# Three weight loads moved from block 1 to block 8 of the first stage

## The chip, the cores and the metric

The kernel runs on one core of one Trainium2 chip. The metric is the time of one execution on the device, in microseconds. A run also leaves a profile of one execution, from which all rows below come. The engines are called as the profile calls them: PE (matmuls; PEld is its weight load), DVE (vector), ACT (scalar activation), POOL (GpSimd) and SP (SyncE), whose only work here is to issue DMAs.

## What is computed

The reference is the sum of an input `x` (2048 tokens of 512, bf16), a sliding-block attention and a gated MLP that mixes tokens, both on the same normalized `x`:

```python
xn = _layernorm(x)
# attention, 32 heads of 16, window of 256 tokens
q, k, v = split(xn @ wqkv)
p = softmax(where(mask, q @ k.T * 16 ** -0.5, -1e9))
a = (p @ v) @ wo
# gated MLP
z = gelu(xn @ w_in)                  # 2048 x 1376
z1, z2 = z[..., :688], _layernorm(z[..., 688:])
g = w_sp @ z2 + b_sp[:, None]        # mixes the 2048 tokens
out = x + a + (z1 * g) @ w_out
```

The bias is `b_sp` (2048 values), `wo` is 512x512, and `w_out` is 688x512.

## The kernel before

The 2048 tokens are 16 blocks of 128 rows (`n` from 0 to 15; `b` is the group of four blocks, `j` the place in the group). There are two stages.

The first stage is the loop over `n` at L392. For each block, PE makes the two halves of `z` (`z_half`, L325, matmuls at L333) from the transposed normalized input `xnT`, and some units of the q, k, v projection (`qkv_unit`, L124, matmuls at L131 and L149, tiles `pj_o` and `pj_f`). ACT applies the gelu and copies q and k out; DVE does the layer-norm statistics (`bn_stats`), normalizes (`ln_apply`, L286 to L293, giving `xn`), copies v out and normalizes `z2`. `xnT` is made by `transposes` (L311 and L312): one transposing DMA for each block, issued by SP, which reads `xn` and writes the block's columns of `xnT`. Four buffers hold `xn`. Blocks 0 to 3 of `xnT` are also needed early and are partly made on PE; from block 4 on PE reads what the DMA wrote.

The second stage runs from an order written out by hand (`ORDER`, L61): token mixing (`gf`, L496), attention scores and products (`S`, L641 and L584), and the output products `fo`, six with `w_out_sb` (L531) and four with `wo_sb` (L538) for each block. The bias is used there as `b_all`, a float copy of `b_bf` made at L441 at the end of the first stage.

Every engine runs its instructions in program order, and SP too: a DMA that waits, for its input or for the queue, holds all DMAs behind it. Completion semaphores for DMAs are eight lanes used in turn, so a DMA also waits until the one eight places ahead has landed. SP's order in the first stage is: the inputs and `w_in`, `x` of blocks 4 to 7 and `wqkv`; transposes of blocks 0, 1, 4 and 5; then, in `load_late` (L223), called once in block 1, `x` of blocks 8 to 15, the bias, `wo` and the first 640 rows of `w_out`; transposes of 6 and 7 (called in block 3); the last 48 rows of `w_out` (L235, in `setup_late`, called in block 4, behind a DVE memset of that chunk); then transposes of 8 and 9 (block 6), 10 and 11 (block 7), 12 and 13 (block 10), 14 and 15 (block 11). The next DMAs are the first loads of the second stage (L477).

The bias load reads 2048 values of 2 bytes so that token `n*128 + p` goes to partition `p`, column `n`:

```python
nc.sync.dma_start(out=b_bf[:], in_=B_b_sp.rearrange("(n p) -> p n", p=P))
```

Of the kernel before, what the change touches and what calls it, by code (L numbers as in the profile page):

```python
# [75 lines left out]
def kernel(  # L76
# [12 lines left out]
    nc = tc.nc  # L89
# [12 lines left out]
    w_out_sb = pers.tile([P, NFC, D], BF, name="w_out_sb")  # L102
# [21 lines left out]
    def qkv_unit(b, i, k):  # L124
        t0 = b * 512
        pt = bank(k)
        if i < 8:
            G, isk = divmod(i, 2)
            w0 = isk * D + G * P
            for c in range(NC):  # L130
                nc.tensor.matmul(  # L131
                    pt[:], lhsT=wqkv[:, c, w0 : w0 + P], rhs=xnT[:, c, t0 : t0 + 512],
                    start=(c == 0), stop=(c == NC - 1),
                )
                yield 512
            if isk:
                nc.scalar.copy(out=kT[:, G, t0 : t0 + 512], in_=pt[:])
            else:
                qt = psum["qt"].tile([P, 512], BF, name="qt", bufs=2)
                nc.scalar.copy(out=qt[:], in_=pt[:])  # L140
                for e in range(2):
                    nc.vector.tensor_scalar(  # L142
                        out=qpad[b][:, G, e, :], in0=qt[:],
                        scalar1=hmask[:, e : e + 1], scalar2=None, op0=ALU.mult,
                    )
        else:
            m = 4 * b + i - 8
            for c in range(NC):
                nc.tensor.matmul(  # L149
                    pt[:], lhsT=xnT[:, c, m * P : (m + 1) * P], rhs=wqkv[:, c, 2 * D : 3 * D],  # L150
                    start=(c == 0), stop=(c == NC - 1),
                )
                yield 512
            nc.vector.tensor_copy(
                out=v_y[:, m, 0 : H * VW].rearrange("p (h w) -> p h w", w=VW)[:, :, 0:DH],
                in_=pt[:].rearrange("p (h d) -> p h d", d=DH),
            )
# [4 lines left out]
    with ExitStack() as actx:  # L162
# [13 lines left out]
        def load_x(eng, n0, n1):  # L176
            b, j = divmod(n0, 4)
            eng.dma_start(
                out=xts[b][:, j : j + n1 - n0, :],
                in_=x2[n0 * P : n1 * P, :].rearrange("(j p) d -> p j d", p=P),  # L180
            )
# [22 lines left out]
        def warm_up(k):  # L204
# [13 lines left out]
            out=hmask[:],  # L218
            in_=ident[:].rearrange("p (s e d) -> p e s d", s=4, e=2),
# [3 lines left out]
        def load_late():  # L223
            load_x(nc.sync, 8, 12)
            load_x(nc.sync, 12, 16)
            with nc.allow_non_contiguous_dma(reason="tiny bias gather"):
                nc.sync.dma_start(out=b_bf[:], in_=B_b_sp.rearrange("(n p) -> p n", p=P))
            nc.sync.dma_start(out=wo_sb[:], in_=A_wo.rearrange("(c p) n -> p c n", p=P))
            nc.sync.dma_start(
                out=w_out_sb[:, 0:5, :], in_=B_w_out[0:640, :].rearrange("(c p) n -> p c n", p=P)  # L230
            )

        def setup_late():
            nc.vector.memset(w_out_sb[:, NFC - 1, :], 0.0)
            nc.sync.dma_start(out=w_out_sb[0:48, 5, :], in_=B_w_out[640:688, :])  # L235
            nc.vector.memset(v_y[:, :, H * VW : VROW], 0.0)
            ones = v_y[:, :, 0 : H * VW].rearrange("p m (h w) -> p m h w", w=VW)
            nc.vector.memset(ones[:, :, :, DH : DH + 1], 1.0)
# [3 lines left out]
        for h in range(2):  # L242
            part = slice(h * KB, h * KB + KB)
            nc.gpsimd.affine_select(
                out=maskFD[part, 0, :], in_=maskFD[part, 0, :], pattern=[[-1, KB]],
# [3 lines left out]
                out=maskFD[part, 1, :], in_=maskFD[part, 1, :], pattern=[[1, KB]],  # L249
# [26 lines left out]
        def ln_batch(b0, k):  # L276
            mvt = sm.tile([P, 4, 2], F32, name="mvt")
            for n in range(b0, b0 + k):
                ln_stats(n, b0, mvt)
                if n == b0 + k - 1:  # L280
                    rs = rstd(mvt, k)
                    for m in range(b0, b0 + k):
                        rsx[m] = rs[:, m - b0 : m - b0 + 1]
                yield

        def ln_apply(n, name="xn"):  # L286
            xs = xts[n // 4][:, n % 4, :]
            xn = lt.tile([P, D], BF, name=name, bufs=4 if name == "xn" else EARLY)
            nc.vector.tensor_scalar(  # L289
                out=xn[:], in0=xs, scalar1=mvx[n], scalar2=rsx[n],  # L290
                op0=ALU.subtract, op1=ALU.mult,
            )
            return xn  # L293
# [17 lines left out]
        def transposes(n, xn):  # L311
            nc.sync.dma_start_transpose(out=xnT[:, :, n * P : (n + 1) * P], in_=xn[:])  # L312
# [12 lines left out]
        def z_half(n, half, inside=None):  # L325
            zp = ps_s.tile([P, 2, 512], F32, name="zp", tag="S")
            src = xcT[:, n] if n < EARLY else xnT[:, :, n * P : (n + 1) * P]
            for c in range(NC):
                if c == NC // 2 and inside is not None:
                    inside()  # L330
                for j in range(2):
                    f0 = half * FH + j * HALF
                    nc.tensor.matmul(  # L333
                        zp[:, j, 0:HALF], lhsT=src[:, c, :],
                        rhs=w_in_sb[:, c, f0 : f0 + HALF],
                        start=(c == 0), stop=(c == NC - 1),
                    )
            dst = (z1 if half == 0 else z2n)[:, n, :]
            nc.scalar.activation(  # L339
                out=dst.rearrange("p (j f) -> p j f", j=2),  # L340
                in_=zp[:, :, 0:HALF], func=ACT.Gelu_apprx_tanh,
                scale=rsx[n] if n < EARLY else 1.0,
            )
# [3 lines left out]
        def z_stats(n):  # L347
            if n % 2 == 0:
                zmv[n // 2] = sm.tile([P, 4, 2], F32, name="zmv")
            mvt = zmv[n // 2]  # L350
            st = sm.tile([P, 2, nc.vector.BN_STATS_DIM], F32, name="st2")
            for j in range(2):
                nc.vector.bn_stats(out=st[:, j, :], in_=z2n[:, n, j * HALF : (j + 1) * HALF])  # L353
            nc.vector.bn_aggr(out=mvt[:, n % 2, :], in_=st[:])
            if n % 2 == 1:
                return rstd(mvt, 2)
            return None
# [34 lines left out]
        for n in range(NB):  # L392
            b, j = divmod(n, 4)
            if n > 1:
                z_half(n, 0)
            if n == 4:
                setup_late()
            if b < 3:
                if j < 2:
                    for i, _ in enumerate(ln_batch(4 * b + 4 + 2 * j, 2)):  # L400
                        if n == 1 and i == 0:
                            for k in (4, 5):
                                transposes(k, ln_apply(k))
                            load_late()
                elif n != 2:
                    for m in range(2):
                        k = 4 * b + 4 + 2 * (j - 2) + m
                        transposes(k, ln_apply(k))
            if n >= 1 and n != 3:
                r = z_stats(n - 1)  # L410
                if r is not None:
                    z_rs[n - 1] = r
            ks = "ofof"[: QKV_AT.get(n, 0)]
            if 3 < n < NB - 1:
                for k in ks[0:1]:
                    for _ in qkv_unit(*qkv_list.pop(0), k):
                        pass
                ks = ks[1:]
            z_half(n, 1, inside=(lambda: turn_early(2, xns.pop(2), 1)) if n == 1 else None)
            if n == 1:  # L420
                turn_early(3, xns.pop(3), 1)
            if n == 3:
                for k in ks[0:2]:
                    for _ in qkv_unit(*qkv_list.pop(0), k):
                        pass
                ks = ks[2:]
                z_stats(n - 1)
            if n % 2 == 1 and n >= 3:
                r = z_rs[n - 2]
                z_apply(n - 3, r)  # L430
                z_apply(n - 2, r)
            if n == NB - 1:
                r = z_stats(n)
            for i, k in enumerate(ks):
                for _ in qkv_unit(*qkv_list.pop(0), k):
                    pass
            if n == NB - 1:
                nc.scalar.activation(out=warm[:, 0:4], in_=warm[:, 4:8], func=ACT.Exp)
                z_apply(n - 1, r)
                z_apply(n, r)  # L440
                nc.vector.tensor_copy(out=b_all[:], in_=b_bf[:])  # L441
# [471 lines left out]
```

## Time and profile before

| | us |
|---|---|
| median of 3 runs | 256.01 |
| lowest and highest of them | 255.07, 257.02 |
| the profiled execution | 254.87 |
| its span, first to last instruction | 253.0 |
| PE, ACT, DVE busy in the span | 246.8, 191.2, 178.6 |
| granted PE clock | 1.0 throughout |

The first stage ends for PE around 86 us; the second takes the rest of the span. Rows of a timeline give start and length in us, engine, line and what is written from what; a bracket gives the idle time ahead of the row and what ended it. A row of waits gives who waited for whom, the total, how often and the longest. SPq rows show how long SP was occupied with issuing a DMA, not how long the transfer took; the time to landing is a separate figure.

### The profile page before, as it was taken

The numbers are of one execution on the slowest core, as the hardware profiler recorded it, in microseconds if no ns is written. First come the engines' busy times: TensorE is split into PE (matmuls) and PEld (weight loads), VectorE is DVE, ScalarE is ACT, GpSimd is POOL, SyncE is SP. The second block draws the span as 40 slices with busy tenths as digits, with TensorE's granted clock in tenths as the row PEclk, the third lists the DMA queues.
The fourth block names the chain that finished last, engine by engine and source line by source line (L and its number), as shares of the span: only waits on it lengthen the run. The fifth ranks groups of instructions, "written<-read, shape, count | busy, mean of one in ns | idle before, by whom it ended". The sixth has DMA issues, their size and how long they took to land.

```text
span 253.0 us, 9066 instructions
## 1 busy us (share of the span) xinstructions
PE 246.8 (98%) x4012; PEld 136.1 (54%) x4036; DVE 178.6 (71%) x373; ACT 191.2 (76%) x229; POOL 16.9 (7%) x53
## 2 busy tenths in 40 slices
PE   8999999999999999999999999999999999999995
PEld 3655555555555455555564555546455555556553
DVE  4997997974557738829586955349688766858974
ACT  6756656546446989989789898989988989988900
POOL 3320312111011000000000000000000000000000
PEclk9999999999999999999999999999999999999999
DMA  6998541039102117783944725445724517852452
GB/s 221 393 165 198 149 81 4 5 65 151 32 0 76 36 20 100 147 89 81 159 89 98 176 51 127 89 99 124 136 85 80 141 34 119 158 99 65 34 90 75
DMA packets 68026, 26.16 MB, mean 103 GB/s; under 512 B 57056, under 2 KB 67472, under 8 KB 67984
## 3 DMA queue, kind: packets, MB, share of 16 engines
q1 hardware_dynamic: 67408, 25.12, 49.0%
q8 instruction: 32, 0.52, 0.9%
q10 hardware_dynamic: 576, 0.44, 0.6%
q14 instruction: 10, 0.08, 0.1%
HBM read 8.41 MB, written 2.10 MB: 42 GB/s over the span
## 4 chain that ended last, share of the span: by engine, by line
PE 87%; DVE 6%; DMA 4%; issue 2%; SPq 1%; POOL 0%; POOLq 0%
PE gf L496 32%; PE S L641 11%; PE zp L333 9%; PE S L584 8%; PE fo L531 8%; PE fo L538 5%; PE pj_o L131 5%; PE pj_f L131 4%; PE pj_f L149 3%; DMA xnT<-xn 2%; PE pj_o L149 2%; DMA xt<-in_A_x_dram 2%; DVE stats L259 1%; DVE st L353 1%; DVE xn L289 1%
## 5 line engine op out<-in xcount | busy, mean ns | idle before, releaser
L650 ACT ACTIVATE E<-S 128x1024 bf16<-128x1024 f32 x152 | 141.9, 1018 | 14.4 <-PE S L641 13.5
L496 PE MATMUL gf<-z2n,wspT 128*128 128x344 bf16 x512 | 85.7, 310 | 0.0
L496 PEld LDWEIGHTS <-wspT 128*128 128x128 bf16 x512 | 45.5, 98 | 31.8 <-issue 11.3
L669 DVE TENSOR_TENSOR E<-E,maskFD 128x1024 bf16<-128x1024 bf16 (+2 forms) x48 | 38.2, 810 | 8.3 <-ACT E L650 7.8
L333 PE MATMUL zp<-w_in_sb,xnT 128*128 128x344 bf16 x224 | 36.6, 309 | 0.2 <-DMA xnT<-xn 0.2
L641 PE MATMUL S<-qpad,kT 32*64 32x512 bf16 (+3 forms) x960 | 31.9, 309 | 0.1
L591 DVE STREAM_TRANSPOSE ot<-S 128x1024 f32<-128x1024 f32 x16 | 20.0, 1247 | 14.4 <-PE S L584 14.3
L333 PEld LDWEIGHTS <-xnT 128*128 128x128 bf16 x224 | 21.8, 98 | 14.3 <-DMA xnT<-xn 0.7
L502 DVE SCALAR_TENSOR_TENSOR u<-gf,b_all,z 128x344 bf16<-128x344 f32 x32 | 18.2, 567 | 12.8 <-PE gf L496 11.5
L531 PE MATMUL fo<-w_out_sb,uT 128*128 128x512 bf16 (+2 forms) x90 | 23.3, 366 | 1.0 <-issue 0.6
L641 PEld LDWEIGHTS <-kT 32*64 32x64 bf16 x960 | 10.9, 102 | 21.6 <-issue 20.6
L584 PE MATMUL S<-E,v_y 64*32 64x256 bf16 (+2 forms) x960 | 21.5, 231 | 0.0
L584 PE MATMUL S<-E,vx 64*32 64x256 bf16 (+3 forms) x960 | 21.5, 232 | 0.0
L339 ACT ACTIVATE z<-zp 128x688 bf16<-128x688 f32 x14 | 10.4, 743 | 14.2 <-PE zp L333 14.1
L584 PEld LDWEIGHTS <-vx 64*32 64x32 bf16 x960 | 18.1, 90 | 4.5 <-issue 4.4
L552 DVE TENSOR_TENSOR xo<-fo,xo 128x512 bf16<-128x512 f32 (+2 forms) x17 | 11.1, 654 | 13.0 <-PE fo L538 12.9
L131 PEld LDWEIGHTS <-wqkv 128*128 128x128 bf16 x128 | 12.5, 98 | 12.6
L584 PEld LDWEIGHTS <-v_y 64*32 64x32 bf16 x960 | 18.9, 90 | 0.6 <-issue 0.6
L131 PE MATMUL pj_o<-xnT,wqkv 128*128 128x512 bf16 x71 | 18.9, 379 | 0.2
L142 DVE TENSOR_SCALAR qpad<-qt,hmask 128x512 bf16<-128x512 bf16 x32 | 9.7, 344 | 10.5 <-ACT qt L140 10.5
L339 ACT ACTIVATE z2n<-zp 128x688 bf16<-128x688 f32 x14 | 10.4, 743 | 8.8 <-PE zp L333 8.8
L538 PE MATMUL fo<-wo_sb,oT 128*128 128x512 bf16 (+2 forms) x64 | 16.3, 366 | 0.6 <-issue 0.6
(70 smaller groups left out, 206.4 us busy)
## 6 DMA issues: line engine op xcount, KB each, us to landing
xo<-in_A_x_dram SPq DMA_DIRECT2D x16, 128.0 KB, 3.1
out_dram<-xo SPq DMA_DIRECT2D x15, 128.0 KB, 2.6
vx<-v_y SPq DMA_DIRECT2D x16, 102.0 KB, 2.7
xt<-in_A_x_dram SPq DMA_DIRECT2D x3, 512.0 KB, 6.1
wqkv<-in_A_wqkv_dram SPq DMA_DIRECT2D x1, 1536.0 KB, 9.5
w_in_sb<-in_B_w_in_dram SPq DMA_DIRECT2D x3, 344.0 KB, 4.8
w_out_sb<-in_B_w_out_dram SPq DMA_DIRECT2D x1, 640.0 KB, 5.6
wo_sb<-in_A_wo_dram SPq DMA_DIRECT2D x1, 512.0 KB, 7.8
```

What stands on the lines that cost most here:

```text
L131: nc.tensor.matmul(pt[:], lhsT=wqkv[:, c, w0 : w0 + P], rhs=xnT[:, c, t0 : t0 + 512], start=(c == 0), stop=(c == NC - 1),)
L333: nc.tensor.matmul(zp[:, j, 0:HALF], lhsT=src[:, c, :], rhs=w_in_sb[:, c, f0 : f0 + HALF], start=(c == 0), stop=(c == NC - 1),)
L339: nc.scalar.activation(out=dst.rearrange("p (j f) -> p j f", j=2), in_=zp[:, :, 0:HALF], func=ACT.Gelu_apprx_tanh, scale=rsx[n] if n < EAR ...
L496: nc.tensor.matmul(gf[:, 0:HALF], lhsT=wspT[t][:, c, :], rhs=z2n[:, c, j * HALF : (j + 1) * HALF], start=(c == 0), stop=(c == NB - 1),)
L502: nc.vector.scalar_tensor_tensor(out=u[:, j * HALF : (j + 1) * HALF], in0=gf[:, 0:HALF], scalar=b_all[:, t : t + 1], in1=z1[:, t, j * HALF ...
L531: nc.tensor.matmul(fo[:, 0:w], lhsT=uTs[t][:, ch, :], rhs=w_out_sb[:, ch, c0 : c0 + w], start=(ch == 0), stop=False,)
L538: nc.tensor.matmul(fo[:, 0:w], lhsT=oTs[t // 2][:, c, q0 : q0 + P], rhs=wo_sb[:, c, c0 : c0 + w], start=False, stop=(c == NC - 1),)
L584: nc.tensor.matmul(o[32 * s : 32 * s + 32, h, q0 : q0 + ni * KB], lhsT=v, rhs=Et[part, s, e, c0 : c0 + ni * KB], start=(i == 0), stop=(i = ...
L591: nc.vector.transpose(out=ot[:].rearrange("p h b j -> p (h b j)"), in_=o[:].rearrange("p h c -> p (h c)"))
L641: nc.tensor.matmul(o.rearrange("p (e q) -> p e q", e=2)[:, :, c0 - b0 : c0 - b0 + ni * KB], lhsT=kT[32 * s : 32 * s + 32, 2 * g + h, k0 : ...
L650: nc.scalar.activation(out=Et[:, 2 * i : 2 * i + 2, :, b0 : b0 + w].rearrange("p s e q -> p (s e) q"), in_=S[i][:].rearrange("p s (e q) -> ...
L669: nc.vector.tensor_tensor(out=v, in0=v, in1=mask, op=ALU.mult)
```

## The change

The loads of the bias, of `wo` and of `w_out` go out of `load_late` (called in block 1) into a function `load_weights`, called at the top of block 8 after its first half of `z`. The load of the last 48 rows of `w_out` goes from `setup_late` (block 4) into the same function. The `x` loads of blocks 8 to 15 stay where they were. The memset of the last chunk of `w_out_sb` stays in block 4.

```diff
         def load_late():
             load_x(nc.sync, 8, 12)
             load_x(nc.sync, 12, 16)
+
+        def load_weights():
             with nc.allow_non_contiguous_dma(reason="tiny bias gather"):
                 nc.sync.dma_start(out=b_bf[:], in_=B_b_sp.rearrange("(n p) -> p n", p=P))
             nc.sync.dma_start(out=wo_sb[:], in_=A_wo.rearrange("(c p) n -> p c n", p=P))
             nc.sync.dma_start(
                 out=w_out_sb[:, 0:5, :], in_=B_w_out[0:640, :].rearrange("(c p) n -> p c n", p=P)
             )
+            nc.sync.dma_start(out=w_out_sb[0:48, 5, :], in_=B_w_out[640:688, :])

         def setup_late():
             nc.vector.memset(w_out_sb[:, NFC - 1, :], 0.0)
-            nc.sync.dma_start(out=w_out_sb[0:48, 5, :], in_=B_w_out[640:688, :])
             nc.vector.memset(v_y[:, :, H * VW : VROW], 0.0)
...
             if n == 4:
                 setup_late()
+            if n == 8:
+                load_weights()
             if b < 3:
```

In the built program SP's order is then: `x` of blocks 8 to 15, transposes of 6, 7, 8, 9, 10 and 11, bias, `wo`, `w_out` (two loads), transposes of 12 to 15. The instructions of PE, DVE, ACT and POOL keep their order; DVE gets one more wait at the `b_all` copy and PE two more at the first `fo` group.

## The prediction

> **What bounds the kernel now.** I read the page first, then the list of waits of the matmul engine, then its timeline through the first stage, then the SyncE queue beside it. The page gives busy time by engine, and the chain that ended last by engine:
>
> ```profile
> PE 246.8 (98%) x4012; PEld 136.1 (54%) x4036; DVE 178.6 (71%) x373; ACT 191.2 (76%) x229; POOL 16.9 (7%) x53
> ...
> PE 87%; DVE 6%; DMA 4%; issue 2%; SPq 1%; POOL 0%; POOLq 0%
> ```
>
> PE is busy for 246.8 of 253.0 us. Only what lets PE run without a gap can shorten this kernel, so the waits of PE over the whole span come next (who waited for whom: total us, times, longest us):
>
> ```profile
> PE heat L206 <- PEq L897: 0.8, 1, 0.8
> PE fo L538 <- issue: 0.6, 4, 0.2
> PE fo L531 <- issue: 0.6, 4, 0.2
> PE zp L333 <- DMA xnT<-xn: 0.2, 1, 0.2
> PE pj_f L149 <- issue: 0.2, 1, 0.2
> ```
>
> One wait of the five has a DMA behind it: a z product (L333) waited once, 0.2 us, for a transposing DMA. The timeline of PE shows which (start us, length us; a matmul starts before the one ahead of it has ended):
>
> ```profile
> 22.22 1.03 PE L131 MATMUL pj_o<-xnT,wqkv 128*128 128x512 bf16 x4
> 23.08 1.33 PE L333 MATMUL zp<-w_in_sb,xnT 128*128 128x344 bf16 x8
> ...
> 27.14 1.03 PE L131 MATMUL pj_o<-xnT,wqkv 128*128 128x512 bf16 x4
> 28.34 1.34 PE L333 MATMUL zp<-w_in_sb,xnT 128*128 128x344 bf16 x8 [0.17 <-DMA xnT<-xn]
> ...
> 38.20 1.33 PE L333 MATMUL zp<-w_in_sb,xnT 128*128 128x344 bf16 x8
> ...
> 58.75 1.33 PE L333 MATMUL zp<-w_in_sb,xnT 128*128 128x344 bf16 x8
> ```
>
> The z product at 28.34 is the first of block 6; those at 38.20 and 58.75 are the first of blocks 8 and 12 (counting pairs of z products from block 4 on). The listed idle time, 0.17, understates the loss, because pipelined matmuls overlap in the record. In the undisturbed place four pj matmuls are followed by a z product after 23.08 - 22.22 = 0.86 us; here it takes 28.34 - 27.14 = 1.20 us. The wait costs 1.20 - 0.86 = 0.34 us of PE's time.
>
> **What the change removes.** The SyncE queue (SPq: issue time and its length, not the transfer) before that wait:
>
> ```profile
> 15.69 1.79 SPq L178 DMA_DIRECT2D xt<-in_A_x_dram  x2
> 17.52 0.51 SPq L227 DMA_DIRECT2D b_bf<-in_B_b_sp_dram  x1
> 18.07 4.13 SPq L228 DMA_DIRECT2D wo_sb<-in_A_wo_dram  x1
> 22.25 0.51 SPq L229 DMA_DIRECT2D w_out_sb<-in_B_w_out_dram  x1
> 22.86 2.73 SPq L312 DMA_TRANSPOSE xnT<-xn  x2
> 25.67 0.53 SPq L235 DMA_DIRECT2D w_out_sb<-in_B_w_out_dram  x1
> ```
>
> and the DVE work that feeds the two transposes at 22.86 (blocks 6 and 7), with their time from issue to landing:
>
> ```profile
> 16.69 0.73 DVE L289 TENSOR_SCALAR xn<-xt,mvt,rs 128x512 bf16<-128x512 bf16 x2
> ...
> DMA to landing us min/median/max: 4.4/4.9/5.4
> ```
>
> Their input is ready at 16.69 + 0.73 = 17.42, yet they are issued at 22.86: the queue is held by the bias, w_o and w_out loads, above all for the 4.13 us in which the w_o load stands behind the bias load. Then block 6 takes 5.4 us to land, at 28.3, with the w_o and w_out loads ahead of it. After the change SyncE reaches the transpose as soon as the two x loads are issued, at 15.69 + 1.79 = 17.48. With the slowest landing seen, 5.4 us, block 6 is there at 22.9. PE can ask for it at 27.14 + 0.86 = 28.00. That leaves 5 us, so the 0.34 us goes entirely. It cannot go by more: PE has no other wait there.
>
> Next in line once PE runs 0.34 us earlier is block 8. The transposes of blocks 8 to 11, then of 12 to 15, are these (duration in ns, first and last issue), with the landing times of the first group:
>
> ```profile
> L312 SPq DMA_TRANSPOSE xnT<-xn x4: 1189/1204/1220, 31.8 to 36.2; - x4
> ...
> DMA to landing us min/median/max: 2.4/2.9/4.3
> ...
> L312 SPq DMA_TRANSPOSE xnT<-xn x4: 1189/1205/1221, 49.3 to 55.5; - x4
> ```
>
> Block 8 is issued at 31.8 and landed by 36.1 at the latest; PE wants it at 38.20 - 0.34 = 37.86. It is not late.
>
> **What the change adds in the new place.** The four loads now stand in SyncE's queue between the transposes of block 11 and block 12. The last of the former is issued at 36.2 + 1.2 = 37.4, and the next is not issued before 49.3, because DVE has not made its input: a hole of 11.9 us in the queue. What the loads need (KB, us from issue to landing) and how full the hole is (busy of the engines, clock, DMA share, GB/s):
>
> ```profile
> wo_sb<-in_A_wo_dram SPq DMA_DIRECT2D x1, 512.0 KB, 7.8
> w_out_sb<-in_B_w_out_dram SPq DMA_DIRECT2D x1, 640.0 KB, 5.6
> b_bf<-in_B_b_sp_dram SPq DMA_DIRECT2D x1, 4.0 KB, 6.6
> w_out_sb<-in_B_w_out_dram SPq DMA_DIRECT2D x1, 48.0 KB, 3.4
> ...
> 15.69:28.34 12.65, 12.37 (x67) 6.47 (x67) 10.59 (x33) 7.32 (x12) 2.11 (x3) 1.00 0.97 213
> 37.50:49.30 11.80, 11.75 (x68) 6.64 (x68) 9.23 (x29) 7.07 (x11) 2.07 (x3) 1.00 0.13 11
> ```
>
> Their issue takes 0.51 + 4.13 + 0.51 + 0.53 = 5.68 us at the old price, so SyncE is free at 43.1, 6.2 us before it is needed. Their transfers ran before from 17.52 to 25.67 + 3.4 = 29.07, 11.55 us, in a stretch whose DMA share was 0.97; the hole's share is 0.13, so they should take less. Even at 11.55 us they end at 49.0. If block 12 nevertheless landed as slowly as block 6 did, 49.3 + 5.4 = 54.7, PE wants it at 58.75 - 0.34 = 58.41: 3.7 us to spare. Cost on PE: nothing, hidden by that margin.
>
> Who needs the loads, and from when, is in the lines of the first readers (duration in ns, first and last start):
>
> ```profile
> L441 DVE CAST b_all<-b_bf x1: 166/166/166, 83.2 to 83.2; 128x16 f32<-128x16 bf16 x1
> ...
> L531 PE MATMUL fo<-w_out_sb,uT x90: 219/379/390, 106.7 to 249.7; 128*128 128x512 bf16 x78, 128*128 128x384 bf16 x6, 128*128 128x128 bf16 x6
> ...
> L312 SPq EVENT_SEMAPHORE  x14: 17/17/17, 5.3 to 55.4; - x14
> ```
>
> The bias is 34 us early at 83.2, the weights 57 us early at 106.7. In the built program DVE has one more wait ahead of that cast, and PE two more ahead of its first fo group, all on loads long landed; at the 17 ns that such a wait takes on SyncE, an upper 0.05 us, taken as nothing. The orders of PE, ACT, POOL and DVE are otherwise untouched. The Trainium skill, in "DMA: Bandwidth & Descriptors", section "Rules for kernel authors", says to issue a DMA early, compute, and wait on it late, which speaks against moving loads later; by it the move could only cost, and the two rows of first use put that cost at nothing here.
>
> One thing the trace cannot price is whether heavy transfers hold an engine without a named reason. The nearest row is this one, in the middle of the loads' old place:
>
> ```profile
> 23.05 0.48 DVE L238 MEMSET v_y<- 128x512 bf16 x1 [1.72 <-issue]
> ```
>
> DVE stood 1.72 us here for nothing that the profile shows. PE stood for nothing of the sort while the DMA share was 0.97. So the bounds are 0 and 1.72 us if the like befalls PE at 37 to 49 us; I take 0, as PE's own rows say. Below nothing is excluded: no engine on the path waited for DVE here.
>
> **Sum.** The profiled execution took 254.87 us, 1.87 outside its span; without the wait it is 254.87 - 0.34 = 254.53. PE works almost without a gap from there to the end, so the gain is carried through. The median of the runs, 256.01, is 1.14 above the profiled one; the same step gives 256.01 - 0.34 = 255.67.
>
> **The rivals.**
> *The wait is longer in other runs.* The landing at block 6 varies with traffic, and the median run is 1.14 us longer than the one profiled. For it: this is the one transfer in the trace that PE outruns. Against: nothing ties the spread of the runs, 255.07 to 257.02, to this place. If all 1.14 us sits there, the time is 256.01 - 0.34 - 1.14 = 254.53. Chance 0.16.
> *Blocks 12 and 13 become late.* The moved loads hold SyncE, and the transpose at 49.3 with it. PE loses from the point at which the queue comes free after 58.41 - 5.4 = 53.0, that is, if the loads hold it for 53.0 - 37.4 = 15.6 us instead of 5.68. Held for twice their whole old transfer time, 23.1 us, block 12 is issued at 60.5, lands at 65.9, 7.2 us after PE began with it before, and the kernel takes 256.01 + 7.2 = 263.2. Against it: the emptier hole. Chance 0.03.
> *PE is held by traffic as DVE was.* 255.67 + 1.72 = 257.39. For it stands one row of another engine; against it PE's silence at the full load. The Trainium skill, "Runtime: NRT & Kernel Launch", section "Instruction fetch mechanics", says that each engine streams its instructions through a DMA queue of its own, a page ahead and mostly hidden; by that the price would be nothing, and no row here ties the 1.72 us to such a fetch. Chance 0.06.
> *Nothing moves.* The 0.34 us of PE is made up or given back in the second stage, where ACT is busy for most of the time: 256.01. Chance 0.10.
>
> **How the numbers follow.** The forecast, 255.67, has the remaining 0.65. The range takes in the first rival with its 254.53, the forecast and no change at all, each with some of the spread of a median of such runs, and stops short of the third rival: 254.3 to 256.8. What a measurement of this kernel can tell from no change is about 1%, 2.56 us. Faster by over that (below 253.45) needs the first rival and twice its wait: 0.05. Slower by over that (above 258.57) is the second rival and a doubled third: 0.04. The rest, 0.91, lies within.
>
> **What would show it.** In the profile after, the wait of zp for xnT is gone from PE's list; the transposes of blocks 6 and 7 are issued near 17.5 and landed by 23; the four loads are issued from 37.4 and are through before 49.3; the transpose of block 12 stays at 49; PE's z product of block 6 starts 0.86 us after the pj group ahead of it, and everything behind is some 0.34 us earlier. Wrong would be: a new wait of PE for xnT at block 8 or 12, a wait for w_out_sb or wo_sb at the first fo group, a PE gap by "issue" between 37 and 49 us, or a change of the time over 1% with none of these to be seen.

## The result and the profile after

| | before | after |
|---|---|---|
| median (22 runs each), us | 255.19 | 254.61 |
| lowest, highest, us | 254.60, 257.02 | 254.24, 255.57 |
| the profiled execution, us (its span) | 254.87 (253.0) | 254.58 (252.7) |

The ratio is 0.9971, with a 95% interval of 0.9958 to 0.9985: faster by 0.29%, or 0.74 us (0.38 to 1.07) of 255.19; the two medians differ by 0.58 us. The two profiled executions differ by 0.29 us. The spread of the runs is smaller too: 1.3 us from lowest to highest, where it was 2.4.

The waits of PE over the whole span of the changed kernel (who waited for whom: total us, times, longest us) no longer have a DMA in them:

```profile
PE heat L206 <- PEq L901: 0.8, 1, 0.8
PE fo L535 <- issue: 0.6, 4, 0.2
PE fo L542 <- issue: 0.6, 4, 0.2
PE pj_f L149 <- issue: 0.2, 1, 0.2
```

Its timeline of PE around block 6, and at the first z product of block 12:

```profile
27.15 1.03 PE L131 MATMUL pj_o<-xnT,wqkv 128*128 128x512 bf16 x4
28.02 1.33 PE L335 MATMUL zp<-w_in_sb,xnT 128*128 128x344 bf16 x8
...
58.42 1.33 PE L335 MATMUL zp<-w_in_sb,xnT 128*128 128x344 bf16 x8
```

PE comes to block 6 at the same moment as before (27.15 against 27.14), but the z product follows after 0.87 us instead of 1.20. From there everything is 0.3 us earlier: block 12 starts at 58.42 instead of 58.75, and the span is 252.7 instead of 253.0. Its SyncE queue (time of issuing, not of transfer):

```profile
15.69 1.79 SPq L178 DMA_DIRECT2D xt<-in_A_x_dram  x2
17.59 21.10 SPq L314 DMA_TRANSPOSE xnT<-xn  x6
38.74 0.57 SPq L229 DMA_DIRECT2D b_bf<-in_B_b_sp_dram  x1
39.37 1.08 SPq L230 DMA_DIRECT2D wo_sb<-in_A_wo_dram  x1
40.49 0.51 SPq L231 DMA_DIRECT2D w_out_sb<-in_B_w_out_dram  x1
41.04 0.52 SPq L234 DMA_DIRECT2D w_out_sb<-in_B_w_out_dram  x1
48.95 7.42 SPq L314 DMA_TRANSPOSE xnT<-xn  x4
```

The six transposes are one merged row; block 6 is its first (duration in ns, first and last issue, then the landing):

```profile
L314 SPq DMA_TRANSPOSE xnT<-xn x1: 1202/1202/1202, 17.6 to 17.6; - x1
DMA to landing us min/median/max: 5.4/5.4/5.4
```

It is issued at 17.59 and, 5.4 us later, landed at 23.0. The time to landing is the 5.4 us of before, so block 6 is early only because it is issued 5.27 us earlier (17.59 against 22.86). In the new place the load behind the bias holds the queue for 1.08 us instead of 4.13, and the queue is free at 41.6, over 7 us before block 12 is ready to be issued at 48.95.

### The profile page after: what moved, and what is told of

Read it like the earlier page. It is cut to its first block, busy times and chain, and to the rows that moved or that the text cites. A ratio compares the mean times of both kernels' runs of the same rounds, so it can differ in the third digit from the quotient of the medians.

```text
span 252.7 us, 9066 instructions
## 1 busy us (share of the span) xinstructions
PE 246.7 (98%) x4012; PEld 136.3 (54%) x4036; DVE 178.7 (71%) x373; ACT 191.3 (76%) x229; POOL 17.0 (7%) x53
## 4 chain that ended last, share of the span: by engine, by line
PE 97%; issue 1%; DVE 0%
PE gf L500 32%; PE zp L335 15%; PE S L645 11%; PE S L588 8%; PE fo L535 8%; PE pj_o L131 6%; PE fo L542 5%; PE pj_f L131 4%; PE pj_f L149 3%; PE pj_o L149 2%; PE heat L206 2%; PE tp L319 0%; DVE xo L556 0%; DVE flag L553 0%
## 5 line engine op out<-in xcount | busy, mean ns | idle before, releaser
L588 PE MATMUL S<-E,vx 64*32 64x256 bf16 (+2 forms) x960 | 21.5, 232 | 0.0
```

The lines of the kernel that those rows point to most:

```text
L588: nc.tensor.matmul(o[32 * s : 32 * s + 32, h, q0 : q0 + ni * KB], lhsT=v, rhs=Et[part, s, e, c0 : c0 + ni * KB], start=(i == 0), stop=(i = ...
```

## The experiments

**One half of the move at a time.** Two kernels move only the bias, or only `wo` and `w_out`, to block 8.

```diff
 # only the bias
-            with nc.allow_non_contiguous_dma(reason="tiny bias gather"):
-                nc.sync.dma_start(out=b_bf[:], ...)
...
+            if n == 8: load_weights()      # b_bf only
```

> Only the bias load moves to block 8; w_o and w_out stay ahead of the transposes of blocks 6 and 7. If the hold of SyncE by the 2-byte bias load makes block 6 late: the transpose of block 6 is issued near 18.6 us, lands near 25 to 26 behind 2.1 MB of loads, PE does not wait, and the time is that of the changed kernel (ratio 0.996 to 0.999). If the bytes of the weights make it late: block 6 still lands at 28 or later, PE waits some 0.3 us, ratio 1.000.

```diff
 # only the weights
-            nc.sync.dma_start(out=wo_sb[:], ...)
-            nc.sync.dma_start(out=w_out_sb[:, 0:5, :], ...)
-            nc.sync.dma_start(out=w_out_sb[0:48, 5, :], ...)
...
+            if n == 8: load_weights()      # wo, w_out only
```

> Only w_o and w_out move to block 8; the bias load stays ahead of the transposes of blocks 6 and 7. If the bytes of the weights make block 6 late: it is issued near 22.2 (held by the bias), lands 2.4 to 4.5 us later, near 25 to 26.5, and PE does not wait: ratio 0.996 to 0.999. If the hold by the bias alone makes it late: it lands near 28 and PE waits as before, ratio 1.000.

Bias alone: ratio 0.9959 (0.9943 to 0.9975). Weights alone: 0.9964 (0.9945 to 0.9983). Neither profile has a wait of PE for `xnT`, and both are as fast as the whole move, so either half is enough. The SyncE queue with the bias alone moved, and the landing of its block 6:

```profile
18.33 0.51 SPq L227 DMA_DIRECT2D w_out_sb<-in_B_w_out_dram  x1
18.93 3.92 SPq L314 DMA_TRANSPOSE xnT<-xn  x2
...
DMA to landing us min/median/max: 7.4/7.4/7.4
```

and with the weights alone moved:

```profile
18.24 0.51 SPq L227 DMA_DIRECT2D b_bf<-in_B_b_sp_dram  x1
18.84 19.49 SPq L314 DMA_TRANSPOSE xnT<-xn  x6
...
L314 SPq DMA_TRANSPOSE xnT<-xn x1: 5334/5334/5334, 18.8 to 18.8; - x1
DMA to landing us min/median/max: 7.3/7.3/7.3
```

Block 6 lands at 18.93 + 7.4 = 26.3 and at 18.84 + 7.3 = 26.1, where PE asks for it near 28: some 2 us to spare in each, against 5 with both moved. In both kernels it is issued some 4 us earlier than before (22.86) and takes 2 us longer to land (5.4 before). The second profile missed an expectation. The transpose was not issued at 22.2, held like the `wo` load before; it was issued at once, and its own issue took 5.33 us. In both places the DMA that came next behind the bias took the hold (`wo` with 4.13 us before, the transpose with 5.33 us here), so a long SPq row can be the price of what stands ahead of it.

**The wait made larger.** The kernel before, with the bias loaded three times in the old place.

```diff
                 nc.sync.dma_start(out=b_bf[:], ...)
+                for bm in b_more:          # two tiles that nobody reads
+                    nc.sync.dma_start(out=bm[:], ...)
```

> The kernel before with the bias loaded three times in the old place (two copies into tiles that nobody reads), so that the suspected wait is made larger. By the old hold of 4.13 us or the landing of 3.5 us in the changed kernel, less some 2 us that any load takes, each copy holds the queue for 1.5 to 4.1 us: the transpose of block 6 is issued 3 to 8.2 us later than at 22.86, PE loses that much more, and if PE paces the kernel to its end the time grows by the same 3 to 8.2 us (ratio 1.012 to 1.032). If the loss is made up later in the kernel, PE shows the wait and the time grows by less than half of it.

The ratio is 1.0164 (1.0117 to 1.0211); the six executions took 258.19 to 262.17. Its SyncE queue and PE's timeline at block 6:

```profile
18.66 5.29 SPq L230 DMA_DIRECT2D b_more<-in_B_b_sp_dram  x2
24.00 1.69 SPq L231 DMA_DIRECT2D wo_sb<-in_A_wo_dram  x1
25.73 0.51 SPq L232 DMA_DIRECT2D w_out_sb<-in_B_w_out_dram  x1
26.34 2.82 SPq L315 DMA_TRANSPOSE xnT<-xn  x2
```

```profile
27.57 1.03 PE L132 MATMUL pj_o<-xnT,wqkv 128*128 128x512 bf16 x4
31.99 1.34 PE L336 MATMUL zp<-w_in_sb,xnT 128*128 128x344 bf16 x8 [3.39 <-DMA xnT<-xn]
```

The transpose is issued 3.5 us later, and PE loses 31.99 - 27.57 - 0.86 = 3.56 us there. Nothing of it comes back: from the z product of block 6 to the end of the span are 257.0 - 31.99 = 225.0 us here, 253.0 - 28.34 = 224.7 before and 252.7 - 28.02 = 224.7 after. The profiled execution is one of the shorter ones, 258.76 us; three of the six took 261.0 us or more, which a wait of 3.56 us does not explain, and the section on the hardware comes back to them.

**The loads in another place behind blocks 6 and 7.** The changed kernel with the call in block 5, so that the loads run at 20 to 29 us, ahead of block 8.

```diff
-            if n == 8:
+            if n == 5:
                 load_weights()
```

> The changed kernel with the four loads called in block 5 instead of block 8, so that SyncE issues them right behind the transposes of blocks 6 and 7, near 20 to 26 us, ahead of the transpose of block 8 at 31.8. If only the place behind blocks 6 and 7 matters: no wait of PE for xnT, and the time of the changed kernel (ratio to before 0.996 to 0.999). If the loads cost something by running at 18 to 29 us beside the rest of the stage: the time of before, ratio 1.000, with no wait at block 6.

The ratio is 0.9971 (0.9958 to 0.9984), that of the changed kernel, and PE has no wait for `xnT`. The loads cost nothing by running beside that part of the stage; they cost by standing ahead of block 6.

**The hole in front of block 12 made to overflow.** The changed kernel with twelve more copies of the bias load at block 8.

```diff
                 nc.sync.dma_start(out=b_bf[:], ...)
+                for bm in b_more:          # twelve tiles that nobody reads
+                    nc.sync.dma_start(out=bm[:], ...)
```

> The changed kernel with twelve more copies of the bias load (into tiles that nobody reads) behind the first one at block 8, to make the queue's hole in front of block 12 overflow. Two more copies took 2.9 us of SyncE at the old place, 1.45 us each; thirteen take 18.9 us from 38.7, the weights another 1.1, so the transpose of block 12 is issued near 58.7 instead of 49.0 and lands 2.4 to 5.6 us later, at 61 to 64. PE wants it at 58.4: a wait of 2.7 to 5.9 us, and the time 257 to 260.5. If the margin of the new place is much larger than reckoned (the copies go through faster in the emptier hole, at 0.6 us each), block 12 is issued by 49 as before and the time stays at 254.6.

The time is 265.16 us, the ratio 1.0378 (1.0351 to 1.0405), 4.7 us above the upper end expected. SyncE's queue, then PE's timeline:

```profile
40.03 18.87 SPq L232 DMA_DIRECT2D b_more<-in_B_b_sp_dram  x12
58.94 1.62 SPq L233 DMA_DIRECT2D wo_sb<-in_A_wo_dram  x1
60.61 0.51 SPq L234 DMA_DIRECT2D w_out_sb<-in_B_w_out_dram  x1
61.16 0.52 SPq L237 DMA_DIRECT2D w_out_sb<-in_B_w_out_dram  x1
61.78 5.15 SPq L317 DMA_TRANSPOSE xnT<-xn  x4
```

```profile
58.26 1.03 PE L132 MATMUL pj_f<-xnT,wqkv 128*128 128x512 bf16 x4
67.29 2.48 PE L338 MATMUL zp<-w_in_sb,xnT 128*128 128x344 bf16 x8 [8.01 <-DMA xnT<-xn]
69.56 1.66 PE L132 MATMUL pj_o<-xnT,wqkv 128*128 128x512 bf16 x4
71.05 1.33 PE L338 MATMUL zp<-w_in_sb,xnT 128*128 128x344 bf16 x8
```

The mechanism is the one reckoned, with two terms too small and one left out. Block 12 was issued at 61.78 instead of 58.7: the twelve copies took 18.87 / 12 = 1.57 us each instead of 1.45, 1.4 us more in all, and the weights behind them 61.78 - 58.94 = 2.84 us instead of 1.1, 1.7 us more. Its landing took 5.5 us, within the 2.4 to 5.6 expected. Left out was that after a wait of 8 us PE ran slowly: the step from one z product to the next is 71.05 - 67.29 = 3.76 us, where it was 2.03 before the change (60.78 - 58.75). From the z product of block 12 to the end are 263.7 - 67.29 = 196.4 us here and 252.7 - 58.42 = 194.3 in the changed kernel, so 2.1 us are lost beyond the wait. The section on the hardware shows the clock.

**How much the wait varies.** The kernel before was profiled six more times, once with a timing against itself.

> The kernel before, unchanged, timed against itself; a second profile of it. Theory 1 (the loss at block 6 is one fixed wait of 0.34 us): the profile shows a wait of PE for xnT at block 6 again, with the z product 1.20 us (+-0.05) after the pj group ahead of it. Theory 2 (the wait varies from execution to execution and is longer in most than in the one profiled): the distance differs from 1.20 by more than 0.1 us. Ratio 1.000 by both, within +-0.002.

> The kernel before, a third profile, to see how the wait at block 6 varies. If it varies from execution to execution by the moment at which block 6 lands: the z product stands 0.86 to 2 us after its pj group, and the time is longer by as much as the distance is. If it is fixed: 1.05 to 1.20 us.

> The kernel before, a fourth profile, with the same two expectations as the third: a distance of 0.86 to 2 us that moves with the landing of block 6 and with the time, or a fixed one of 1.05 to 1.20 us.

> The kernel before, a fifth profile. The four so far show losses at block 6 of 0.19 to 0.46 us in executions of 254.69 to 255.70 us, while about a quarter of the timed executions takes 256 to 257.3. If those long ones are long waits at block 6: an execution above 256 shows a distance of over 1.9 us there. If not: the distance stays at 1.05 to 1.35 us, whatever the time, and a long execution has its extra time elsewhere, the first 5 us above all.

> The kernel before, a sixth profile: as the fifth, a distance of over 1.9 us at block 6 in an execution above 256 us if long waits there make the long executions, or 1.05 to 1.35 us whatever the time if they do not.

> The kernel before, a seventh profile: as the fifth, a distance of over 1.9 us at block 6 in an execution above 256 us if long waits there make the long executions, or 1.05 to 1.35 us whatever the time if they do not.

Against itself the kernel has a ratio of 0.9984 (0.9966 to 1.0001): two timings of one kernel differed by 0.4 us here, over half of the gain measured for the change. The profiles (issue of block 6 by SyncE, start of the pj group, start of the z product; the loss is the distance of the last two less 0.86):

| profile of before | time | issue | pj | z | loss |
|---|---|---|---|---|---|
| first | 254.87 | 22.86 | 27.14 | 28.34 | 0.34 |
| second | 254.96 | 22.95 | 27.43 | 28.48 | 0.19 |
| third | 254.69 | 22.77 | 26.92 | 28.23 | 0.45 |
| fourth | 255.70 | 23.69 | 27.84 | 29.16 | 0.46 |
| fifth | 255.46 | 23.27 | 27.62 | 28.80 | 0.32 |
| sixth | 254.93 | 22.94 | 27.00 | 28.37 | 0.51 |
| seventh | 256.32 | 24.28 | 27.69 | 29.78 | 1.23 |

The mean loss is 0.50 us, and 0.38 without the seventh. The second profile, with a distance of 1.05 us, rules out one fixed wait of 0.34, though it is shorter and not longer as its second theory had it. The expectation that the time grows with the distance failed with the third: with a loss of 0.45 us it is the shortest execution of the seven.

Two readings of the table go beyond the losses. From the issue of block 6 to the z product are 5.43 to 5.53 us in all seven, and the landing itself took 5.4 to 5.5 us, so the z product starts when the transpose has landed, and the time to landing hardly varies. The loss varies because SyncE's lead over PE does: the issue stands 4.48 us ahead of the pj group in the second profile, which loses least, and 3.41 us in the seventh, which loses most. And as 224.7 to 224.9 us follow the z product in each, the whole spread of the time among the seven arises ahead of it.

The seventh is the one long execution that a profile caught; its distance of 2.09 us is over the 1.9 expected of long waits. Its SyncE queue and its PE:

```profile
13.79 3.51 SPq L312 DMA_TRANSPOSE xnT<-xn  x2
17.36 1.12 SPq L178 DMA_DIRECT2D xt<-in_A_x_dram  x2
18.53 0.51 SPq L227 DMA_DIRECT2D b_bf<-in_B_b_sp_dram  x1
19.08 4.55 SPq L228 DMA_DIRECT2D wo_sb<-in_A_wo_dram  x1
23.67 0.51 SPq L229 DMA_DIRECT2D w_out_sb<-in_B_w_out_dram  x1
```

```profile
6.30 3.95 PE L333 MATMUL zp<-w_in_sb,xcT 128*128 128x344 bf16 x26 [0.81 <-DMA w_in_sb<-in_B_w_in_dram]
...
27.69 1.03 PE L131 MATMUL pj_o<-xnT,wqkv 128*128 128x512 bf16 x4
29.78 1.34 PE L333 MATMUL zp<-w_in_sb,xnT 128*128 128x344 bf16 x8 [1.06 <-DMA xnT<-xn]
```

Two things make it long. The `w_in` load lands late, so PE comes to block 6 0.55 us later than in the first profile (27.69 against 27.14). And SyncE is later still: it begins the two transposes ahead 0.66 us later (13.79 against 13.13), needs 0.35 us more for them and the `x` loads, and 0.41 us more from the bias to the transpose of block 6, so that block 6 is issued at 24.28, 1.42 us later. PE pays the difference at block 6. From its z product to the end are 254.6 - 29.78 = 224.8 us.

**The changed kernel once more.**

> The changed kernel, a second profile and a second timing on one chip. By the wait alone (0.19 to 0.46 us in the profiles so far): ratio 0.998 to 0.9993, and no wait of PE for xnT, with 0.86 us from the pj group to the z product of block 6. If executions of the kernel before often wait longer there than the profiled ones: ratio 0.995 to 0.9975 again.

The ratio is 0.9974 (0.9962 to 0.9986), in the second of the two ranges expected, though the interval reaches into the first, and there is no wait of PE for `xnT`. Its profiled execution took 254.93 us; PE came to block 6 late as well, and did not wait:

```profile
27.37 1.03 PE L131 MATMUL pj_o<-xnT,wqkv 128*128 128x512 bf16 x4
28.23 1.33 PE L335 MATMUL zp<-w_in_sb,xnT 128*128 128x344 bf16 x8
```

Of the 0.35 us by which this execution is longer than the first profile of the changed kernel, 0.2 are that late start (28.23 against 28.02); the rest lies behind block 6.

## Why the prediction was right, and where its size was off

*The wait goes, and with it 0.34 us of the profiled execution.* Right. The distance from the pj group to the z product fell by 0.33 us, the span by 0.3 and the time by 0.29. Reading the loss from the distance of two starts, not from the listed idle time of 0.17, gave the right number; the second profile of before lists no wait at all where 0.19 us was lost.

*The time, 255.67.* The measured 254.61 lies in the range, 1.06 us below the forecast. Of these, 0.82 us are the starting point: 256.01 was the median of three runs, and over 22 runs the kernel before has 255.19. The other 0.24 are the difference of the medians, 0.58 instead of 0.34. That the time came out beside the 254.53 of the first rival is luck: that sum takes 1.48 us off a median that was too high.

*It is carried through to the end.* Right, and the tripled bias shows it over a tenfold range: 224.6 to 225.0 us follow the z product of block 6 in every profile in which PE does not wait later.

*Block 6 lands by 22.9, 5 us early.* Right: 23.0. The 5.4 us to landing are the same as before, though `wo` and `w_out` no longer stand ahead of it, so the move gained nothing in the landing itself. The two half moves show that the wait came from the bias and the weights together, each worth more than the 0.34 us that was missing.

*The new place is free.* Right, and freer than reckoned. The issue of the four loads took 0.57 + 1.08 + 0.51 + 0.52 = 2.68 us instead of 5.68, though they began at 38.74 and not at 37.4. The stretch's DMA share was 0.13 before the change, against 0.97 in the old place; that this is the reason was not tried by itself. The rival in which blocks 12 and 13 become late is a real mechanism, shown by the thirteen copies; four loads are far from the 15.6 us of hold that the prediction gave as its condition.

*It cannot go by more, as PE has no other wait there.* This is the term that was mis-sized for the runs as a whole. In that one execution it holds, but the wait differs from execution to execution: 0.19 to 1.23 us in seven, 0.50 in the mean. The measured gain, 0.74 us with 0.38 to 1.07, holds 0.50 and, at its lower end, not 0.34; but as two timings of one kernel differed by 0.4 us, it is the seven profiles that show the wait to vary, not the timing. So the first rival, longer waits in other runs, was right in part. Its reason, that the landing varies with traffic, does not hold among these seven: the landing took 5.4 to 5.5 us in each, and what varied is the moment of issue against PE's arrival. Its price was too high too: it put all of the 1.14 us between the profiled execution and the median of three there, while a part of the spread is a late start of PE, which the change leaves. The medians over more runs stand 0.25 to 0.65 us above the first profile, not 1.14.

*PE held by traffic as DVE was.* Not seen. DVE's unexplained stop stayed, ahead of the same memset, with the four loads gone from its neighbourhood, so they were not its cause:

```profile
23.06 0.48 DVE L240 MEMSET v_y<- 128x512 bf16 x1 [1.71 <-issue]
```

What is its cause was not tried.

*Nothing moves.* Excluded by both timings of the change, whose intervals end at 0.9985 and 0.9986, and by the 0.3 us by which everything behind block 6 starts earlier in the profile.

What stays open is whether waits like the seventh profile's make all of the long executions of before; one such execution was profiled. Open too is how much of the 0.74 us is the wait: its mean of 0.50 comes from seven profiles, three of them taken to find a long execution.

## What to carry to other kernels

In an in-order DMA queue, put loads that are needed late behind the transfers that the matmul engine needs next, and look for a hole in the queue where the next transfer's input is not ready anyway. The bias here is 4 KB, read as 2-byte elements, and the DMA behind it took 4.13 us to issue: look at what stands ahead of a long issue. A wait of 0.2 us in one profile is an edge, not a size: compare when the transfer is issued and how long it takes to land with when the reader comes, in several profiles, before pricing it.

## What the runs showed of the hardware

A 4 KB bias gather of 2048 single elements took 6.6 us to land behind the `x` loads and 3.5 us where the changed kernel has it, but back to back it cost the queue 1.57 us a copy.

A long wait of PE can cost more than the wait. With the thirteen copies, the windows around the wait (busy time of PE, PEld, DVE, ACT, POOL, then the granted PE clock, DMA share, GB/s) are:

```profile
56.00:58.00 2.00, 2.00 (x12) 1.02 (x11) 1.35 (x4) 1.34 (x3) 0.00 (x0) 1.00 0.76 2
...
68.00:70.00 2.00, 2.00 (x9) 0.92 (x7) 0.00 (x0) 0.20 (x1) 0.00 (x0) 0.50 1.28 77
70.00:72.00 2.00, 2.00 (x11) 1.04 (x10) 0.09 (x1) 1.13 (x2) 0.00 (x0) 0.79 0.79 175
72.00:74.00 2.00, 1.95 (x11) 0.96 (x11) 0.53 (x2) 1.33 (x2) 0.00 (x0) 1.00 1.02 213
```

When PE came back at 67.29 after 8 us without work, the clock was granted at half, and it stayed so until near 70.8 (a mean of 0.79 over 70 to 72 is half for 0.84 us of the two). With the tripled bias the profiled execution waited 3.4 us, kept a clock of 1.0 and lost no more than its wait. Three of its six executions had a mean clock of 1.0 over the run and took 258.2 to 258.8 us; the other three had 0.986 to 0.992 and took 261.0 to 262.2, and none of these was profiled. The Trainium skill, "TensorE: Matmul & The Clock Gate", section "Part 1: The HAM clock gate (the "warmup" mystery)", says that the clock goes to half after at least one idle window of about 3.4 us. The thirteen copies agree with that (8.0 us, 0.50); the tripled bias, with a wait of 3.4 us and the clock kept, lies at that edge, and no run here shows where the threshold is. In the kernel before, the longest loss seen was 1.23 us, and the clock around it was 1.00.
